# Longer fixed times for VectorE and ScalarE and a shorter one for GpSimd in the plan that orders an attention and rational-FFN kernel

## The chip, the cores and the metric

The kernel runs on one core of one Trainium2 chip. The metric is the device time of one execution in microseconds (us); the median of the runs is compared.

## The reference, cut to what matters

```python
def sm_attn(qq, kk, vv):                       # softmax attention, scale 1/sqrt(64)
    s = scale * np.matmul(qq, kk.transpose(0, 1, 3, 2))
    s = s - np.max(s, axis=-1, keepdims=True)
    a = np.exp(s)
    a = a / (np.sum(a, axis=-1, keepdims=True) + 1e-09)
    return np.matmul(a, vv)
p_packed = sm_attn(p, k, v)                    # q, k, v: 8 x 8 x 576 x 64; p: 8 x 8 x 32 x 64
out = sm_attn(q, p_packed, p_packed)
x = out.transpose(0, 2, 1, 3).reshape(4608, 512)
h = x @ w_in                                   # 512 x 2048
P = a[0] + a[1] * h + a[2] * h * h + a[3] * h * h * h
Q = 1.0 + np.abs(b[0]) * np.abs(h) + np.abs(b[1]) * h * h
g = P / (Q + 1e-6)
return g @ w_out                               # 2048 x 512
```

`q`, `k`, `v` and `p` are float32; the weights `w_in` and `w_out` come as float64 and go in as their 64-bit words.

## The kernel before

**How the work is cut.** The feed-forward part is cut into 128 units: batch (8), half of the batch's 576 rows (2 x 288), chunk of 256 of the 2048 hidden columns (8). In the names of tiles the unit's number stands in the middle: `Y0_115_1398` is buffer 0 of ring `Y` as unit 115 uses it; a name's last number counts all tiles. For each unit, `hidden` computes h into two PSUM banks (`h0`, `h1`), with twelve 128x288 matmuls from `AH`/`AL` (the attention's result, split into a high and a low float32r part) and `m`. ScalarE reads each bank three times: `Y` (a3 h + a2), `U` (|b h|) and `sq` (the square). VectorE then turns `Y` into the numerator with a multiply and a scalar-tensor-tensor (stt) per bank; the second of them is the last reader of the bank. GpSimd adds `sq` to `U`; ScalarE takes Ln and Exp of it (`V`, 1/Q); VectorE does three 128x576 operations to get g in `Y`; ScalarE casts it to `gh`, GpSimd subtracts for `gl`, and copies the columns of the batch's last rows to `G`. Three units later `acc_block` multiplies `gh`, `gl` with `w_out` (`w`) in twelve 128x512 matmuls into `acc`, whose sums leave through `o` every eight units. `remainder` does the rows in `G`.

**What lies between.** The attention of the next batch, and its `m_chunk` (`at<-win,ppT`, 16 small matmuls, then a ScalarE cast and a VectorE subtraction `m<-at,m`), are spread over the units as filler. The attention keeps its working tile in `kx`, a ring with one buffer: `kx<-nat` (VectorE transposes) brings k of the next batch into it, and the last reads of the previous batch are ScalarE's `AH<-kx` and GpSimd's `AL<-kx`. In the first units (up to about the tenth, "early") the weights' words are still being converted: VectorE `o<-o` operations on 128x1024 words, then a ScalarE cast and a GpSimd subtraction to `w`. Rings that matter here: `h` 2 banks in all (so unit n+1's h waits for unit n's stt on the same bank), `Y` 3, `U` 2, `sq` 1, `kx` 1, `o` 1, `at` 2.

**What sets the order.** Nothing is issued where it is written. Class `Planner` records all 7086 operations (`PlannedEngine`), finds from the tiles what must come before what (`edges`), and plans start times by list scheduling (`schedule`), with rounds that go through the program backwards to set each operation's rank; of 4 rounds the plan that ends first is kept (`order`). `issue` (line 216) then emits the operations by planned start. So almost every instruction has line 216, and each engine works its own list strictly in that order. A planned duration is `fixed + per * columns` by engine (`cost`), with the pair taken from `COST`:

```python
        fixed, per = self.COST[engine]
        ...
        return fixed + per * self.columns(aps[1] if name.startswith("reduce") else aps[0])
```

Of the kernel before, what the change touches and what calls it, by code (L numbers as in the profile page):

```python
# [31 lines left out]
class Planner:  # L32
# [4 lines left out]

    ENGINES = ("tensor", "vector", "scalar", "gpsimd", "sync")

    COST = {"vector": (70, 1.04), "scalar": (93, 0.83), "gpsimd": (215, 2.11), "tensor": (15, 0.417)}  # L40
    TRANSPOSE, F32 = (15, 0.834), (30, 1.667)
    WAY = {("vector", "vector"): 127, ("scalar", "scalar"): 143, ("tensor", "tensor"): 0, ("gpsimd", "gpsimd"): 0}
    WAY.update({(f"sync", x): 0 for x in ENGINES})
# [32 lines left out]
    def cost(self, engine, name, args, kwargs):  # L76
        if engine == "sync":
            return self.DMA_ISSUE
        fixed, per = self.COST[engine]
        if engine == "tensor":  # L80
# [875 lines left out]
```

## Time and profile before

| | |
|---|---|
| time, median of 3 runs | 804.35 us (803.67 to 804.96) |
| the profiled execution's own time | 803.09 us |
| its span | 801.3 us |
| mean granted TensorE clock | 0.97 of full speed |
| PE (TensorE matmul) busy | 745.9 us, 93% |
| DVE (VectorE) busy | 706.9 us, 88% |
| ACT (ScalarE) busy | 671.3 us, 84% |
| POOL (GpSimd) busy | 460.7 us, 57% |

The profile is one execution on the chip. Engine names are those of the table; busy time is the time in which at least one instruction of the engine is under way, and a share is of the span. The span leaves out what lies around it, 1.8 us here. A row of a timeline gives the start, the time, the engine, the operation with out<-in, and in brackets how long the engine stood idle before it and whose result ended the wait. Rows of one kind that follow each other closely are joined (x2 and more).

### The profile page before, as it was taken

The page shows a single profiled execution, that of the slowest core. Times are in us where ns is not written, and L with a number is a line of the kernel's source. Part 1 is how long each engine was busy: PE and PEld are TensorE (multiplying, and loading weights), DVE is VectorE, ACT ScalarE, POOL GpSimd, SP SyncE. Part 2 cuts the span into 40 slices and gives each one's busy share as a digit, 9 for nine tenths or more (in the row PEclk, how much of TensorE's full clock was granted, in tenths as well). Part 3 has the DMA queues.
Part 4 walks back from the last instruction along what each step waited for, and adds up shares of the span by engine and source line. Part 5 has one row for each costly group of instructions (what it writes and reads, how often), then busy time and mean ns, then how long its engine had stood idle before and what let it go on. Part 6 is the DMA issues. An engine that isn't in the chain of part 4 may idle for free.

```text
span 801.3 us, 15242 instructions
## 1 busy us (share of the span) xinstructions
PE 745.9 (93%) x5440; PEld 588.2 (73%) x5440; DVE 706.9 (88%) x1308; ACT 671.3 (84%) x1494; POOL 460.7 (57%) x462
## 2 busy tenths in 40 slices
PE   5587686899999999999999999999999999999997
PEld 4255464678878788678877888778877887778886
DVE  2999999898899789998899789998899789998883
ACT  5899988789888798889888798889788798998972
POOL 0006455565577555756568455855578555866663
PEclk9668899899999999999999999999999999999999
DMA  7983135002730208110720219010910123000001
GB/s 251 387 251 134 58 114 80 27 5 79 88 66 1 83 15 114 39 56 27 105 49 3 82 27 129 12 57 27 118 35 26 54 38 64 1 1 26 27 1 41
DMA packets 152029, 56.05 MB, mean 70 GB/s; under 512 B 122256, under 2 KB 141200, under 8 KB 151952
## 3 DMA queue, kind: packets, MB, share of 16 engines
q1 hardware_dynamic: 151952, 55.07, 29.9%
q8 instruction: 43, 0.70, 0.4%
q14 instruction: 34, 0.28, 0.1%
HBM read 45.62 MB, written 9.44 MB: 69 GB/s over the span
## 4 chain that ended last, share of the span: by engine, by line
PE 71%; DVE 12%; ACT 10%; DMA 3%; POOL 2%; issue 2%; SPq 1%; DVEq 0%
PE acc L216 36%; PE h L216 23%; PE at L216 13%; DVE Y L216 6%; ACT Y L216 2%; DVE w L216 2%; ACT m L216 1%; DMA w<-in_q_dram 1%; ACT U L216 1%; DVE small L216 1%; ACT V L216 1%; ACT w L216 1%; DVE V L216 1%; POOL gl L216 1%; ACT sq L216 1%
## 5 line engine op out<-in xcount | busy, mean ns | idle before, releaser
L216 PE MATMUL acc<-w,gh 128*128 128x512 f32 x1024 | 328.2, 402 | 9.9 <-ACT w L216 5.0
L216 PEld LDWEIGHTS acc<-w,gh 128*128 128x128 f32 x1024 | 185.6, 190 | 61.2 <-issue 9.7
L216 POOL TENSOR_TENSOR U<-U,sq 128x576 f32<-128x576 f32 x118 | 169.1, 1433 | 81.4 <-ACT U L216 52.1
L216 PE MATMUL h<-AH,m 128*128 128x288 f32 x1024 | 189.1, 306 | 13.6 <-DVE Y L216 12.5
L216 POOL TENSOR_TENSOR gl<-Y,gh 128x512 fp32r<-128x512 f32 x128 | 168.2, 1314 | 48.1 <-ACT gh L216 19.6
L216 PE MATMUL acc<-w,gl 128*128 128x512 f32 x512 | 192.2, 397 | 0.0
L216 PEld LDWEIGHTS h<-AH,m 128*128 128x128 f32 x1024 | 160.3, 193 | 43.3 <-DVE Y L216 29.2
L216 ACT ACTIVATE Y<-h,abS 128x288 f32<-128x288 f32 x256 | 125.1, 507 | 19.5 <-PE h L216 13.6
L216 DVE TENSOR_TENSOR Y<-Y,h 128x288 f32<-128x288 f32 x256 | 109.9, 445 | 27.3 <-ACT Y L216 9.9
L216 ACT ACTIVATE sq<-h 128x288 f32<-128x288 f32 x236 | 97.8, 416 | 42.4 <-PE h L216 33.7
L216 DVE SCALAR_TENSOR_TENSOR Y<-Y,abS,h 128x288 f32<-128x288 f32 x256 | 125.1, 506 | 2.3
L216 DVE SCALAR_TENSOR_TENSOR Y<-Y,abS,V 128x576 f32<-128x576 f32 x128 | 103.0, 805 | 22.5 <-ACT V L216 21.9
L216 PEld LDWEIGHTS acc<-w,gl 128*128 128x128 f32 x512 | 96.6, 189 | 27.9 <-issue 8.4
L216 PE MATMUL h<-AL,m 128*128 128x288 f32 x512 | 111.5, 299 | 0.0
L216 ACT ACTIVATE U<-h 128x288 f32<-128x288 f32 x256 | 98.6, 421 | 12.2 <-PE h L216 5.9
L216 POOL COPY G<-Y 128x64 f32<-128x64 f32 x128 | 32.2, 251 | 129.8 <-DVE Y L216 120.4
L216 ACT ACTIVATE V<-U,one 128x576 f32<-128x576 f32 x128 | 97.8, 764 | 5.3 <-DVE Y L216 5.1
L216 DVE SCALAR_TENSOR_TENSOR Y<-V,Y 128x576 f32<-128x576 f32 x128 | 95.8, 748 | 2.0
L216 DVE SCALAR_TENSOR_TENSOR V<-U,V 128x576 f32<-128x576 f32 x128 | 96.1, 751 | 0.0
L216 ACT CAST gh<-Y 128x512 fp32r<-128x512 f32 x128 | 80.9, 632 | 6.7 <-DVE Y L216 5.9
L216 ACT ACTIVATE V<-V 128x576 f32<-128x576 f32 x128 | 84.4, 660 | 0.5
L216 PEld LDWEIGHTS h<-AL,m 128*128 128x128 f32 x512 | 84.2, 192 | 0.2
(124 smaller groups left out, 828.3 us busy)
## 6 DMA issues: line engine op xcount, KB each, us to landing
out_dram<-o SPq DMA_DIRECT2D x15, 512.0 KB, 2.8
w<-in_moe_w_out_dram SPq DMA_DIRECT2D x14, 512.0 KB, 4.5
nat<-in_k_dram SPq DMA_DIRECT2D x48, 144.0 KB, 3.9
nat<-in_q_dram SPq DMA_DIRECT2D x48, 144.0 KB, 4.4
nat<-in_v_dram SPq DMA_DIRECT2D x24, 256.0 KB, 3.7
m<-in_moe_w_in_dram SPq DMA_DIRECT2D x8, 512.0 KB, 9.8
w<-in_moe_w_in_dram SPq DMA_DIRECT2D x8, 512.0 KB, 11.3
nat<-in_k_dram SPq DMA_DIRECT2D x4, 512.0 KB, 7.5
```

The lines of the kernel that those rows point to most:

```text
L216: getattr(getattr(self.nc, engine), name)(*args, **kwargs)
```

## The change

One line differs: the fixed part of the planned duration rises from 70 to 100 ns for VectorE and from 93 to 121 ns for ScalarE, and falls from 215 to 170 ns for GpSimd.

```diff
--- before.py
+++ after.py
@@ -37,7 +37,7 @@
 
     ENGINES = ("tensor", "vector", "scalar", "gpsimd", "sync")
 
-    COST = {"vector": (70, 1.04), "scalar": (93, 0.83), "gpsimd": (215, 2.11), "tensor": (15, 0.417)}
+    COST = {"vector": (100, 1.04), "scalar": (121, 0.83), "gpsimd": (170, 2.11), "tensor": (15, 0.417)}
     TRANSPOSE, F32 = (15, 0.834), (30, 1.667)
     WAY = {("vector", "vector"): 127, ("scalar", "scalar"): 143, ("tensor", "tensor"): 0, ("gpsimd", "gpsimd"): 0}
     WAY.update({(f"sync", x): 0 for x in ENGINES})
```

The recorded operations and what depends on what are the same in both kernels; so are the tile numbers. What differs is the order in which each engine has its instructions. Three places:

**VectorE, units 10 to 12, while the last weight words are converted** (`o0_2_263<-o0_2_263`, three rows; `kx` and `small` are the attention's, `m0_9` the early `m_chunk`'s). Before (the two transposes `kx0_2_141<-at0_49_278` and `kx0_2_141<-at1_50_279` stand right ahead of these rows, and the third `o` row right behind them):

```order
L216 SCALAR_TENSOR_TENSOR Y0_10_253<-Y0_10_253,abS_68,V0_10_252 128x576
L216 TENSOR_REDUCE small_73<-kx0_2_141 128x18
L216 SCALAR_TENSOR_TENSOR V0_10_252<-U1_10_251,V0_10_252 128x2x288
L216 SCALAR_TENSOR_TENSOR Y0_10_253<-V0_10_252,Y0_10_253 128x576
L216 TENSOR_TENSOR m0_9_298<-at0_51_299,m0_9_298 128x512
L216 TENSOR_TENSOR Y2_12_282<-Y2_12_282,h0_23_284 128x288
L216 TENSOR_REDUCE small_73<-kx0_2_141 128x18
L216 TENSOR_SCALAR o0_2_263<-o0_2_263 128x512
L216 TENSOR_TENSOR Y2_12_282<-Y2_12_282,h1_24_287 128x288
L216 SCALAR_TENSOR_TENSOR o0_2_263<-o0_2_263 128x512
L216 SCALAR_TENSOR_TENSOR Y2_12_282<-Y2_12_282,abS_68,h0_23_284 128x288
```

After:

```order
L216 SCALAR_TENSOR_TENSOR Y0_10_253<-Y0_10_253,abS_68,V0_10_252 128x576
L216 TENSOR_SCALAR o0_2_263<-o0_2_263 128x512
L216 SCALAR_TENSOR_TENSOR V0_10_252<-U1_10_251,V0_10_252 128x2x288
L216 SCALAR_TENSOR_TENSOR o0_2_263<-o0_2_263 128x512
L216 SCALAR_TENSOR_TENSOR Y0_10_253<-V0_10_252,Y0_10_253 128x576
L216 ISA o0_2_263<-o0_2_263,full0_3_264 128x512x2
L216 TENSOR_TENSOR Y2_12_282<-Y2_12_282,h0_23_284 128x288
L216 TENSOR_REDUCE small_73<-kx0_2_141 128x18
L216 SCALAR_TENSOR_TENSOR Y2_12_282<-Y2_12_282,abS_68,h0_23_284 128x288
L216 TENSOR_TENSOR Y2_12_282<-Y2_12_282,h1_24_287 128x288
L216 SCALAR_TENSOR_TENSOR Y1_11_267<-Y1_11_267,abS_68,V0_11_266 128x576
L216 SCALAR_TENSOR_TENSOR Y2_12_282<-Y2_12_282,abS_68,h1_24_287 128x288
```

The three `o` rows now stand between the last operations of unit 10; one of the two `small` reductions, the `m0_9` subtraction and the two transposes stand behind the operations of unit 12 shown here, where before they stood ahead of unit 12's first stt.

**VectorE, units 94 to 97, where k of the next batch comes in** (`kx0_8_1222<-nat`: four transposes into the one `kx` buffer). Before:

```order
L216 TENSOR_TENSOR Y2_96_1198<-Y2_96_1198,h0_191_1200 128x288
L216 TENSOR_TENSOR Y2_96_1198<-Y2_96_1198,h1_192_1201 128x288
L216 SCALAR_TENSOR_TENSOR Y2_96_1198<-Y2_96_1198,abS_68,h0_191_1200 128x288
L216 SCALAR_TENSOR_TENSOR Y2_96_1198<-Y2_96_1198,abS_68,h1_192_1201 128x288
L216 TENSOR_TENSOR full0_6_1184<-at0_169_1205,full0_6_1184 128x512
L216 SCALAR_TENSOR_TENSOR Y1_95_1187<-Y1_95_1187,abS_68,V0_95_1186 128x576
L216 STREAM_TRANSPOSE kx0_8_1222<-nat0_39_1118 128x576
L216 SCALAR_TENSOR_TENSOR V0_95_1186<-U0_95_1185,V0_95_1186 128x2x288
L216 STREAM_TRANSPOSE kx0_8_1222<-nat1_40_1129 128x576
L216 SCALAR_TENSOR_TENSOR Y1_95_1187<-V0_95_1186,Y1_95_1187 128x576
L216 TENSOR_TENSOR Y0_97_1208<-Y0_97_1208,h0_193_1210 128x288
L216 STREAM_TRANSPOSE kx0_8_1222<-nat0_39_1118 128x576
```

After:

```order
L216 STREAM_TRANSPOSE kx0_8_1222<-nat0_39_1118 128x576
L216 SCALAR_TENSOR_TENSOR Y1_95_1187<-Y1_95_1187,abS_68,h0_189_1189 128x288
L216 TENSOR_TENSOR Y1_95_1187<-Y1_95_1187,h1_190_1190 128x288
L216 STREAM_TRANSPOSE kx0_8_1222<-nat1_40_1129 128x576
L216 SCALAR_TENSOR_TENSOR Y1_95_1187<-Y1_95_1187,abS_68,h1_190_1190 128x288
L216 STREAM_TRANSPOSE kx0_8_1222<-nat0_39_1118 128x576
L216 TENSOR_TENSOR m1_30_1193<-at0_167_1194,m1_30_1193 128x512
L216 SCALAR_TENSOR_TENSOR Y0_94_1176<-Y0_94_1176,abS_68,V0_94_1175 128x576
L216 TENSOR_TENSOR m1_30_1193<-at1_168_1195,m1_30_1193 128x512
L216 SCALAR_TENSOR_TENSOR V0_94_1175<-U1_94_1174,V0_94_1175 128x2x288
L216 STREAM_TRANSPOSE kx0_8_1222<-nat1_40_1129 128x576
L216 SCALAR_TENSOR_TENSOR Y0_94_1176<-V0_94_1175,Y0_94_1176 128x576
```

The four transposes stood behind unit 96's operations on its `h` banks, the first of them behind both; now all four stand ahead of those (which follow as the next four rows), between unit 95's. At unit 64 all four have moved in the same way, at unit 32 three of the four. On GpSimd the second of the two subtractions `AL0_7_1136<-kx0_7_1046,AH0_9_1135`, which the first transpose waits for, now stands ahead of `gl0_93` and unit 95's addition `U0_95`; before, both stood behind those.

**ScalarE, unit 115, in the last batch.** Before:

```order
L216 ACTIVATE sq0_105_1399<-h0_229_1400 128x288
L216 ACTIVATE sq0_105_1399<-h1_230_1402 128x288
L216 ACTIVATE Y0_115_1398<-h0_229_1400,abS_68 128x288
L216 ACTIVATE Y0_115_1398<-h1_230_1402,abS_68 128x288
L216 ACTIVATE U0_115_1396<-h0_229_1400 128x288
L216 ACTIVATE U0_115_1396<-h1_230_1402 128x288
```

After:

```order
L216 ACTIVATE sq0_105_1399<-h0_229_1400 128x288
L216 ACTIVATE Y0_115_1398<-h0_229_1400,abS_68 128x288
L216 ACTIVATE sq0_105_1399<-h1_230_1402 128x288
L216 ACTIVATE Y0_115_1398<-h1_230_1402,abS_68 128x288
L216 ACTIVATE U0_115_1396<-h0_229_1400 128x288
L216 ACTIVATE U0_115_1396<-h1_230_1402 128x288
```

The square of the second bank stood ahead of the first bank's `Y`; now it stands behind it. Units 116 and 118 to 124 have the same exchange, unit 117 has not.

## Rows read from the trace of the kernel before

**Rows 1.** The page: busy time of each engine (us, share of the span, instructions), and one row of the costliest groups (busy us, mean ns of one, idle time before it).

```profile
PE 745.9 (93%) x5440; PEld 588.2 (73%) x5440; DVE 706.9 (88%) x1308; ACT 671.3 (84%) x1494; POOL 460.7 (57%) x462
...
L216 DVE TENSOR_TENSOR Y<-Y,h 128x288 f32<-128x288 f32 x256 | 109.9, 445 | 27.3 <-ACT Y L216 9.9
```

**Rows 2.** Busy time by stretch: PE, PEld (weight loads), DVE, ACT, POOL busy us (x instructions), the granted TensorE clock, the share of the DMA engines, GB/s.

```profile
100.00:150.00 50.00, 37.87 (x310) 27.40 (x308) 48.39 (x90) 40.68 (x82) 27.58 (x26) 0.93 0.37 78
150.00:200.00 50.00, 50.00 (x347) 41.20 (x348) 45.76 (x89) 43.91 (x105) 31.77 (x35) 1.00 0.14 44
584.00:607.00 23.00, 22.33 (x129) 18.08 (x128) 21.71 (x41) 21.28 (x48) 19.30 (x20) 1.00 0.06 24
705.00:755.00 50.00, 49.20 (x271) 41.46 (x264) 43.84 (x78) 43.66 (x102) 30.98 (x33) 1.00 0.03 11
```

**Rows 3.** The same view of two stretches of 10 us.

```profile
130.00:140.00 10.00, 4.96 (x51) 2.86 (x49) 9.97 (x18) 8.73 (x20) 5.74 (x7) 0.98 0.11 44
140.00:150.00 10.00, 6.36 (x35) 4.44 (x35) 8.43 (x16) 5.91 (x13) 5.17 (x5) 0.68 0.01 2
```

**Rows 4.** The chain of waits that ended last, followed inside 100 to 150 us: start, us, what.

```profile
141.76 0.43 DVE Y L216
...
142.24 2.53 PE h L216 x9
```

**Rows 5.** PE's timeline, 132 to 151 us.

```profile
134.95 1.09 PE L216 MATMUL at<-win,ppT 64*32 64x512 f32 x16
142.24 1.33 PE L216 MATMUL h<-AH,m 128*128 128x288 f32 x4 [6.20 <-DVE Y L216]
...
146.27 1.11 PE L216 MATMUL at<-win,ppT 64*32 64x512 f32 x16
...
149.91 0.73 PE L216 MATMUL acc<-w,gh 128*128 128x512 f32 x2 [1.40 <-ACT o L216]
```

**Rows 6.** VectorE's timeline, 126 to 152 us.

```profile
133.45 0.84 DVE L216 STREAM_TRANSPOSE kx<-at 128x288 f32<-128x288 f32 x2
...
134.91 0.74 DVE L216 TENSOR_REDUCE small<-kx 128x18 f32<-128x576 f32 x1
...
137.02 0.68 DVE L216 TENSOR_TENSOR m<-at,m 128x512 fp32r<-128x512 f32 x1
...
140.12 0.44 DVE L216 TENSOR_TENSOR Y<-Y,h 128x288 f32<-128x288 f32 x1
...
142.11 0.68 DVE L216 CUSTOM_DVE_ANT_0 o<-o,full 128x1024 uint16<-128x1024 uint16 x1
...
148.11 0.69 DVE L216 TENSOR_TENSOR m<-at,m 128x512 fp32r<-128x512 f32 x1 [1.50 <-ACT m L216]
...
150.44 0.81 DVE L216 SCALAR_TENSOR_TENSOR Y<-Y,abS,V 128x576 f32<-128x576 f32 x1 [0.36 <-ACT V L216]
```

**Rows 7.** VectorE's timeline, 603 to 618 us.

```profile
607.42 0.69 DVE L216 TENSOR_TENSOR m<-at,m 128x512 fp32r<-128x512 f32 x1 [0.71 <-ACT m L216]
...
611.25 0.82 DVE L216 TENSOR_TENSOR Y<-Y,h 128x288 f32<-128x288 f32 x2 [0.15 <-ACT U L216]
611.99 0.93 DVE L216 SCALAR_TENSOR_TENSOR Y<-Y,abS,h 128x288 f32<-128x288 f32 x2
...
614.16 0.77 DVE L216 STREAM_TRANSPOSE kx<-nat 128x576 f32<-128x576 f32 x1
614.86 0.73 DVE L216 SCALAR_TENSOR_TENSOR V<-U,V 128x576 f32<-128x576 f32 x1
```

**Rows 8.** PE's timeline in the same stretch: the first `h` matmuls of unit 97.

```profile
613.74 0.69 PE L216 MATMUL h<-AH,m 128*128 128x288 f32 x4
```

**Rows 9.** GpSimd's timeline in the same stretch.

```profile
607.57 2.84 POOL L216 TENSOR_TENSOR AL<-kx,AH 128x576 fp32r<-128x576 f32 x2
```

**Rows 10.** PE's timeline, 505 to 536 us: two waits.

```profile
522.15 0.73 PE L216 MATMUL acc<-w,gh 128*128 128x512 f32 x2 [0.45 <-ACT gh L216]
...
532.48 0.80 PE L216 MATMUL h<-AH,m 128*128 128x288 f32 x4 [0.36 <-DVE Y L216]
```

**Rows 11.** The timeline of all engines in the last batch, 713 to 725 us; 714.30 and 719.08 are the first `h` matmuls of units 115 and 116.

```profile
714.30 0.79 PE L216 MATMUL h<-AH,m 128*128 128x288 f32 x4
...
715.46 0.41 ACT L216 ACTIVATE sq<-h 128x288 f32<-128x288 f32 x1 [0.55 <-PE h L216]
...
716.18 0.41 ACT L216 ACTIVATE sq<-h 128x288 f32<-128x288 f32 x1 [0.30 <-PE h L216]
...
716.49 0.89 ACT L216 ACTIVATE Y<-h,abS 128x288 f32<-128x288 f32 x2
...
717.25 0.72 ACT L216 ACTIVATE U<-h 128x288 f32<-128x288 f32 x2
...
717.78 0.82 DVE L216 TENSOR_TENSOR Y<-Y,h 128x288 f32<-128x288 f32 x2 [0.56 <-ACT U L216]
...
718.51 0.93 DVE L216 SCALAR_TENSOR_TENSOR Y<-Y,abS,h 128x288 f32<-128x288 f32 x2
...
719.08 0.80 PE L216 MATMUL h<-AH,m 128*128 128x288 f32 x4 [0.19 <-DVE Y L216]
```

**Rows 12.** PE's timeline in the same stretch: the first `h` matmuls of unit 117.

```profile
723.29 0.73 PE L216 MATMUL h<-AH,m 128*128 128x288 f32 x4
```

**Rows 13.** PE's timeline, 750 to 760 us: the first `h` matmuls of unit 124.

```profile
755.70 0.81 PE L216 MATMUL h<-AH,m 128*128 128x288 f32 x4 [0.21 <-DVE Y L216]
```

## Prediction

> **What bounds the kernel now.** I read the busy times first, then the stretches, then the chain of waits, then the timelines of the places where the new order differs. The page shows PE busy for 93% of the span and VectorE for 88% [rows 1]. That average hides two regimes [rows 2]. From 100 to 150 us VectorE is busy for 48.39 of 50 us and PE for 37.87: VectorE sets the pace there. From 150 to 200 us PE is busy for all 50 us and VectorE has 4 us to spare, and later stretches look alike: 22.33 of 23 us from 584 to 607, 49.20 of 50 from 705 to 755. So after 150 us an earlier VectorE or ScalarE result is worth at most the idle time of PE that it ends, and a later one costs nothing until it eats the slack in front of PE. The change alters no instruction, only orders, so the sum is one of waits: which of PE's waits shrink, which appear.
>
> **The start (term A).** From 130 to 150 us PE works 4.96 and 6.36 us of each 10 us [rows 3], and the chain that ended last runs through VectorE up to the stt at 141.76, then through unit 13's h [rows 4]. Those h matmuls come after the longest wait here, 6.20 us for VectorE [rows 5]. The order now puts ahead of that stt: one reduction less (0.74), the subtraction m0_9 less (0.68), one multiply of the other bank less (0.44), the two transposes less (0.84), and the third conversion row more (0.68) [rows 6]. That is 2.70 - 0.68 = 2.02 us; each instruction starts about 0.08 us before the end of the one ahead (two multiplies take 0.82 us, and the next row starts 0.73 us after their start [rows 11]), and with four instructions fewer it is about 1.7 us. So h of unit 13 should start near 140.5 instead of 142.24.
>
> I don't count all of that. The instructions taken out from in front stand behind, before unit 14's first operation or soon after it, and from there VectorE has the same work behind it as before. What lasts is VectorE's idle time that the new order fills: 1.50 us in front of a subtraction m at 148.11, which waits for ScalarE's cast and now stands further back, and 0.36 us at 150.44 [rows 6]. That gives 1.9 us. The bounds: at best the 1.7 us, the 1.50 us and PE's 1.40 us wait at 149.91 [rows 5] all stay, 4.6 us; at worst nothing stays and the two groups of m_chunk matmuls, 1.09 and 1.11 us, which lay in PE's idle time (134.95) or beside it (146.27) [rows 5] and which the new order puts behind the accumulations of units 9 and 10, fall into PE's full stretch, +2.2. I take -1.9, near the middle.
>
> With PE's clock it goes the same way: it is granted 0.68 of full speed, between 1.2 and 2.4 GHz, in the ten microseconds with the 6.20 us wait, against 0.98 in the ten before [rows 3]; a wait of 4.5 instead of 6.2 us may leave it there or not, and I count nothing for it.
>
> **The transposes of k (term B).** Each takes 0.70 us of VectorE from its start to the next one's [rows 7], four are 2.8 us. Before, they lay behind unit 96's stt on its first bank, which ends about 611.99 + 0.51 = 612.50 (two with an overlap of 0.08 us take 0.93, so one (0.93 + 0.08) / 2), and unit 97's h starts at 613.74 [rows 7, 8]: slack 1.24 us. Now they lie ahead of it. They also fill VectorE's gaps at 607.42 (0.71) and 611.25 (0.15) [rows 7]. So PE's new wait is 2.8 - 0.86 - 1.24 = 0.7 us. A second wait can come on top: `kx` has one buffer, and the first transpose waits for GpSimd's second AL. Before, the pair of ALs took 607.57 to 610.41 [rows 9], over 3.7 us ahead of the first transpose at 614.16; now the transpose stands right behind unit 95's first multiply, ahead of the subtraction at 607.42 [rows 7] and so at least 6.7 us earlier, while the second AL is moved ahead of gl0_93 and unit 95's addition only, and unit 95's remaining h operations queue behind it. I bound that wait by nothing and by one AL, 2.84 / 2 = 1.42 us. A place thus costs 0 to 2.1 us, and I take 1.0. Units 64 and 96 have it; at unit 32 the fourth transpose stays behind, which leaves 2.1 - 0.86 - 1.24 = 0. Two places: +2.0, from 0 to +4.2; with the AL wait at all three, +5.6.
>
> **Waits that go (term C).** In units 77 to 82 and 45 to 50, the same transposes and m subtractions stand further back, behind unit operations. PE's two real waits there are 0.45 us for `gh` and 0.36 us for a VectorE result [rows 10], together 0.81, and 1.6 for both places. Units 84 to 86 get more VectorE work ahead in return, so I take half: -0.8, from -1.6 to 0.
>
> **The last batch (term D).** Units start 4.60 us apart (714.30 to 755.70, nine units), and the shortest spacing with the same matmuls, 719.08 to 723.29, is 4.21: 0.39 us per unit are not PE's own work [rows 11 to 13]. ScalarE waits 0.30 us at 716.18 for the second bank's h before its square, and only then does the two Ys and the two Us; the multiply at 717.78 waits 0.56 us for U, and 719.08 waits for VectorE [rows 11]. The new order does the first bank's Y in that gap (two take 0.76 us, from 716.49 to 717.25). So Y and U end 0.30 us earlier. Nine units have the exchange; where the spacing is already 4.2 nothing can come of it. Nine times 0.30 is 2.7, and I take a little over half: -1.5, from -2.7 to 0.
>
> **Does the table come nearer to the engines?** A 128x288 multiply lasts 445 ns in the mean [rows 1], and two of them with the next start take 0.73 us, 0.365 each [rows 11]. The old plan has 70 + 1.04 x 288 = 370 ns, the new one 400. As a length of a result the new number is nearer, as a length of occupation the old one is. A rule of the Trainium skill speaks here against the change ("Perfetto Trace Analysis", section "DVE / Act Engine Instruction"): the profiler's duration runs until the write is acknowledged, while the next instruction may begin to fetch when execution ends, so recorded durations overstate what an engine is held for. The trace agrees by the two numbers above. By it the new plan sees about 1308 x 30 ns = 39 us of VectorE work that isn't there, and its order is a redraw with no better aim: net zero, 804.35.
>
> **The sum**, against the profiled execution's own 803.09: -1.9 + 2.0 - 0.8 - 1.5 = -2.2, 800.9. The median shown is 1.26 above that execution, so I give the median as 802.1. A difference under about 0.2% (1.6 us) can't be told from no change.
>
> **Rivals.**
> - Nothing net: where PE is the bound, waits only change places. A falls to +0.3 (the m_chunk matmuls on PE's path take back the filled idle time, -1.9 + 2.2), C to 0, B and D stay: +0.8, 805.1; or, as a redraw, 804.35. For it: PE is full from 150 us on [rows 2]. Against it: PE's idle time in the last batch is real and has one cause.
> - Slower: the transposes wait for GpSimd's AL with VectorE's queue behind them, at all three places, 2.1 us each: +6.3 instead of +2.0, the other terms as forecast, +2.1, 806.5. It decides when a place costs more than 4.2 / 3 = 1.4 us. For it: VectorE is busy 21.71 of the 23 us ahead of the place [rows 2] and cannot absorb a wait. Against it: gaps of 0.86 us right behind [rows 7].
> - A larger gain: the start keeps its whole 4.6 us and D its 2.7: -4.6 + 2.0 - 0.8 - 2.7 = -6.1, 798.2. For it: the chain really runs through that stt. Against it: VectorE's later work is unchanged.
>
> **How the numbers follow.** Forecast 40%, its own range 800.5 to 803; larger gain 13%; nothing net 24%; slower 23%. The likeliest is 802.1. The range 797 to 808 reaches to both outer cases. Faster by over 0.2% (below 802.7): four fifths of the forecast's share and the larger gain, 0.45; slower by over 0.2% (above 806.0): the slower rival and some of nothing net, 0.27; the same 0.28.
>
> **What would show it.** A: the wait of 6.20 us before unit 13's h falls below 5, VectorE's 1.50 us gap ahead of the subtraction is gone, and PE is full from about 148. B: a wait of unit 97's h for VectorE, 0.5 to 2 us, and a VectorE wait for GpSimd's AL ahead of the first transpose, or none. C: no waits over 0.3 us where unit 77 to 82 run. D: ScalarE's Y ahead of its second square, and a mean spacing near 4.45 us from unit 115 to 124. The prediction is wrong if PE shows new waits in places that I haven't read, such as the first 100 us, where the orders differ most, or behind unit 125, where the last batch drains.

## The result and the profile after

The changed kernel is slower: 809.75 us (median of 6 runs, 808.47 to 811.29) against 804.71 of the kernel before in the same session, a ratio of 1.0069 with a 95% interval of 1.0057 to 1.0081, so about 5.5 us. The profiled execution took 809.4 us with a span of 807.5, 6.2 above the span of before. PE's busy time has grown by 2.8 us [rows 1], and the time in which it isn't busy by 3.4:

```profile
PE 748.7 (93%) x5440; PEld 588.4 (73%) x5440; DVE 705.2 (87%) x1308; ACT 668.9 (83%) x1494; POOL 467.1 (58%) x462
```

**Where PE waits behind 150 us.** The first block is the view of waits of the changed kernel, from 150 to 760 us, the second that of before: who waited for whom, us in total, times, the longest.

```profile
PE h L216 <- DVE Y L216: 8.9, 21, 0.8
PE acc L216 <- ACT gh L216: 1.2, 2, 0.6
PE at L216 <- POOL o L216: 0.8, 3, 0.3
```

```profile
PE h L216 <- DVE Y L216: 3.0, 9, 1.0
PE acc L216 <- ACT gh L216: 2.6, 7, 0.5
PE acc L216 <- ACT o L216: 1.4, 1, 1.4
```

PE's waits for a VectorE result in front of h have gone from 9 to 21 and from 3.0 to 8.9 us. The waits for `gh` have halved. The one for ScalarE's `o` (1.40 us, [rows 5]) ended at 149.91; the view lists it because its matmuls run past 150, and it belongs to the start. Without it the listed waits come to 5.6 us before and 10.9 after. They are small in the changed kernel, 0.2 to 0.8 us each, and those for h are spread from unit 20 to unit 118.

**The start.** The stretches 0 to 150, 50 to 100, 100 to 130 and 130 to 150 us, first of the changed kernel, then of before (columns as in [rows 2]):

```profile
0.00:150.00 150.00, 106.63 (x834) 75.04 (x835) 126.93 (x224) 121.07 (x240) 55.25 (x49) 0.85 0.56 170
50.00:100.00 50.00, 36.47 (x255) 24.24 (x254) 47.82 (x76) 46.15 (x96) 25.88 (x18) 0.82 0.38 121
100.00:130.00 30.00, 24.56 (x196) 19.57 (x195) 30.00 (x54) 23.57 (x49) 16.53 (x12) 0.94 0.40 96
130.00:150.00 20.00, 14.94 (x99) 11.36 (x98) 18.44 (x36) 16.07 (x37) 11.85 (x12) 0.91 0.30 56
```

```profile
0.00:150.00 150.00, 105.40 (x861) 74.37 (x861) 129.80 (x232) 123.89 (x245) 50.16 (x51) 0.84 0.55 170
50.00:100.00 50.00, 37.65 (x261) 27.84 (x262) 47.69 (x77) 45.93 (x97) 21.58 (x18) 0.82 0.38 122
100.00:130.00 30.00, 26.55 (x226) 20.10 (x225) 30.00 (x58) 26.04 (x51) 16.67 (x15) 1.00 0.58 115
130.00:150.00 20.00, 11.32 (x86) 7.30 (x84) 18.39 (x33) 14.64 (x32) 10.91 (x11) 0.83 0.06 23
```

From 130 to 150 PE works 14.94 us instead of 11.32. But from 100 to 130 it works 24.56 instead of 26.55, with its clock granted at 0.94 instead of 1.00, and from 50 to 100 it works 1.2 us less. Over all 150 us it is busy for 1.2 us longer, and has yet begun fewer matmuls, 834 against 861.

### The profile page after: what moved, and what is told of

The parts are those of the page before. It is cut to its first block, busy times and chain, and to the rows that moved or that the text cites. A ratio compares the mean times of both kernels' runs of the same rounds, so it can differ in the third digit from the quotient of the medians.

```text
span 807.5 us, 15287 instructions
## 1 busy us (share of the span) xinstructions
PE 748.7 (93%) x5440; PEld 588.4 (73%) x5440; DVE 705.2 (87%) x1308; ACT 668.9 (83%) x1494; POOL 467.1 (58%) x462
## 4 chain that ended last, share of the span: by engine, by line
PE 57%; DVE 19%; ACT 12%; DMA 4%; issue 4%; SPq 2%; POOL 2%; DVEq 0%; POOLq 0%; ACTq 0%
PE acc L216 28%; PE h L216 18%; PE at L216 11%; DVE Y L216 9%; ACT Y L216 2%; ACT V L216 2%; DVE w L216 2%; SPq L216 2%; DVE kx L216 2%; DVE small L216 2%; DVE V L216 2%; ACT U L216 2%; ACT sq L216 2%; DMA w<-in_moe_w_in_dram 1%; DMA w<-in_moe_w_out_dram 1%
## 5 line engine op out<-in xcount | busy, mean ns | idle before, releaser
L216 PE MATMUL acc<-w,gh 128*128 128x512 f32 x1024 | 319.9, 401 | 10.4 <-ACT w L216 8.4
L216 DVE TENSOR_TENSOR Y<-Y,h 128x288 f32<-128x288 f32 x256 | 108.1, 445 | 39.3 <-ACT U L216 28.0
L216 DVE SCALAR_TENSOR_TENSOR Y<-Y,abS,h 128x288 f32<-128x288 f32 x256 | 122.9, 504 | 1.5
L216 POOL COPY G<-Y 128x64 f32<-128x64 f32 x128 | 40.9, 320 | 115.1 <-DVE Y L216 106.0
L216 ACT ACTIVATE U<-h 128x288 f32<-128x288 f32 x256 | 96.9, 425 | 4.1 <-DVE V L216 2.3
```

The source lines that it names most:

```text
L216: getattr(getattr(self.nc, engine), name)(*args, **kwargs)
```

## The experiments

All times are ratios of the runs to the runs of before that were taken with them, with 95% intervals; 0.1% is 0.8 us. "Span" is that of the one profiled execution (801.3 for before).

**One number at a time.** Three tables, each with one of the three numbers changed.

```diff
-    COST = {"vector": (70, 1.04), "scalar": (93, 0.83), "gpsimd": (215, 2.11), ...
+    COST = {"vector": (100, 1.04), "scalar": (93, 0.83), "gpsimd": (215, 2.11), ...   # e1_vector
+    COST = {"vector": (70, 1.04), "scalar": (121, 0.83), "gpsimd": (215, 2.11), ...   # e2_scalar
+    COST = {"vector": (70, 1.04), "scalar": (93, 0.83), "gpsimd": (170, 2.11), ...    # e3_gpsimd
```

> Only VectorE's fixed time goes from 70 to 100 ns. Theory one (the loss comes from where VectorE's other work now stands in front of the operations that free h banks, so it is VectorE's number that decides): most of the change's +5 us, 807 to 810. Theory two (the loss comes from ScalarE's order, whose other work now stands between its reads of an h bank): near before, 803 to 806. Theory three (no part decides; each new table draws another order and the old one happened to be a good draw): any time between 800 and 812, and no sum over the three parts.

Measured: 1.0023 (1.0013 to 1.0033).

> Only ScalarE's fixed time goes from 93 to 121 ns. Theory one (VectorE's number): near before, 803 to 806. Theory two (ScalarE's number): 807 to 810, with VectorE waiting for ScalarE's U as in the changed kernel. Theory three (a draw): anything from 800 to 812.

Measured: 1.0025 (1.0016 to 1.0035).

> Only GpSimd's fixed time goes from 215 to 170 ns. Theories one and two: near before, 803 to 806, since GpSimd is busy for 58% and its number is now nearer to its pace. Theory three (a draw): anything from 800 to 812, and again other than the rest of the change would leave.

Measured: 1.0041 (1.0028 to 1.0055). No number carries the loss alone, and the one that I took for harmless costs most. That speaks against the first two theories. The sum of the three, 0.89% where the whole is 0.69%, decides nothing: the intervals allow the two to be equal. The later runs test the third theory directly.

**The start alone, and everything but the start.** Both plans are made in one kernel, and the order is taken from one of them up to the first h matmul of unit 17, then from the other.

```diff
     def issue(self):
-        for i in self.order():
+        plans = {}
+        plans["old"] = self.order()
+        self.COST = self.NEW
+        plans["new"] = self.order()
+        head, tail = plans["new"], plans["old"]      # e4_head_new; e11_head_old: the other way round
...
+        head = head[: at[0]]                         # at[0]: the first operation on h0_33
+        done = set(head)
+        for i in head + [i for i in tail if i not in done]:
```

> The changed kernel's order up to the first h matmul of unit 17 (about 170 us), the order of before from there. If the start is a third of the loss, as unit 17 starting 1.8 us later in the changed kernel suggests: 806 to 807. If the later start is only PE work that was done ahead (PE was busy 1.2 us longer in the first 150 us of the changed kernel): 804.5 to 805.5. If my forecast of a gain at the start held: 802 to 803.5.

Measured: 1.0015 (1.0005 to 1.0025), span 802.9, 1.6 above before. From unit 20 to the end the distance of this run to the one before stays at 1.5 to 1.7 us, since every engine then does the same in the same order. One span doesn't size the start: executions whose order is still that of before reach unit 14 from 1.0 us earlier (e11_head_old) to 0.8 later (e12_swap) than the profiled one of before. The times do: the start is a real loss, of 1.2 us (0.4 to 2.0).

> The order of before up to unit 17, the changed kernel's from there: the rest without the start. The whole is 5.5 us and the start alone 1.2, so 4.3 above before if the two add up: 808 to 809.5. If the seam costs or gives work of its own, as it did in the mixed order: off by up to 3 us.

Measured: 1.0074 (1.0060 to 1.0089), span 805.7, 4.4 above before. By the spans start and rest add up (1.6 + 4.4 = 6.0 of 6.2); by the times they come to 7.1 of 5.5, which their intervals just allow. Most of the loss lies behind unit 17.

**The last batch alone.** The same edit with the order of before up to unit 114 (`h0_227`) and the changed one from there.

> The order of before up to the first h matmul of unit 114 (about 710 us), the changed kernel's order from there: term D alone. My forecast was -1.5 us, so 802. The traces of the two kernels say that the changed one loses about 1.1 us behind unit 113: 804.5 to 805.

Measured: 0.9995 (0.9986 to 1.0004), span 801.5. The last batch as a whole neither gains nor loses: neither number was right. Units 115 to 124 stand 4.67 us apart in this run against 4.60 before, and what that costs is made up behind unit 124.

**The exchange on ScalarE alone.** The order of before, and in units 115 to 124 ScalarE's reads of h in the sequence of the changed kernel.

```diff
...
+        for n in range(115, 125):
+            own = [k for k, i in enumerate(row) if self.unit(self.ops[i][1][0]) == n]
+            for k, i in zip(own, sorted((row[k] for k in own), key=at.get)):
+                row[k] = i
```

> The order of before, with ScalarE's exchange alone in units 115 to 124 (the first bank's Y ahead of the second bank's square). My term D as it was argued: 1.5 us faster, 802 to 803, with units 4.4 us apart. If the Y waits for its buffer, whose last reader is GpSimd's gl three units back, as the changed kernel's trace says: no gain, 803.5 to 805, ScalarE waiting about 0.2 us for gl ahead of Y.

Measured: 1.0010 (1.0002 to 1.0019), no gain. The view of ScalarE's waits from 700 to 760 us, the two largest groups of this run and the largest of before:

```profile
ACT sq L254 <- PE h L254: 4.2, 9, 0.6
ACT Y L254 <- POOL gl L254: 2.0, 7, 0.4
```

```profile
ACT sq L216 <- PE h L216: 5.7, 13, 0.6
```

The wait for GpSimd's `gl`, which the kernel before doesn't have there at all, has come with this exchange alone. Its 2.0 us take back the 1.5 that the squares wait less.

**Stretches of different plans put together.** In the run of e2_scalar the distance to before shrank from 5.3 us at unit 17 to 0.4 at unit 113. So I took that plan between the two, and the order of before at both ends.

```diff
+    PIECES = [('old', 'h0_33'), ('sca', 'h0_225'), ('old', None)]   # 'sca': ScalarE at 121
...
```

> The order of before up to unit 17, the order of the plan with ScalarE's number alone (121) up to unit 113, the order of before behind it. In that plan's own run the distance to before fell from 5.3 us at unit 17 to 0.4 at unit 113. If what a stretch costs stays with its order (as the head's 1.6 us did), this one is 4.9 us faster than before: 798 to 799.5. If the gain was only catching up with a late start, nothing is left of it: 803 to 804.

Measured: 1.0044 (1.0030 to 1.0058), slower than either of its parts. The reading behind it was wrong: this run too is 4.1 us behind at unit 17 and 0.8 at unit 105, and then 4.4 at unit 113, at the seam. When unit 17 starts says how much attention work PE has done by then as well as how late it is. What a plan does early it needn't do later, and a seam pays the difference. The start of a unit measures lost time only where both orders have done the same work up to it, as behind unit 20 in e4_head_new.

**No other work inside the h chain.** On ScalarE and VectorE, from unit 17 on, whatever stands between a unit's first and last operation on its h banks goes behind the last one, where the dependences allow; in the changed kernel, and in the one before.

```diff
+                part = row[own[0] : own[-1] + 1]
+                new = [i for i in part if u[i] == n] + [i for i in part if u[i] != n]
...
+                tried = {**lists, e: row[: own[0]] + new + row[own[-1] + 1 :]}
+                if self.merged(tried, order):
+                    lists = tried
```

> The changed kernel's order, and from unit 17 on all that ScalarE and VectorE have between a unit's first and last operation on its h banks is put behind the last one, wherever the dependences allow. If PE's new waits for VectorE come from other work standing inside that chain: most of the 4.3 us behind unit 17 is back, 805 to 806.5. If they come from how PE's own filler is spread over the units, or the order is one draw among many: still 808 to 812.

Measured: 1.0591 (1.0575 to 1.0606).

> The same rule on the order of before, which has more such work inside the chain (154 rows on ScalarE and 134 on VectorE, against 94 and 79 in the changed one). If that work costs time: faster than before, 800 to 803. If what is pushed back is missed as badly elsewhere: 804 to 810.

Measured: 1.0696 (1.0677 to 1.0714). Both are over 47 us slower. PE's waits in e9_gather_new from 150 to 800 us, the three largest groups:

```profile
PE h L259 <- DVE Y L259: 10.2, 15, 2.2
PE at L259 <- DVE kx L259: 6.4, 5, 1.6
PE at L259 <- ACT kx L259: 5.4, 5, 1.4
```

The waits for h haven't even fallen (10.2 us in 15 waits, the longest 2.2), and others have come, for the attention's transposes and exponentials. So other work inside the chain is not in itself the loss: moving it out costs far more than the change studied, and the kernel before, which has more of it, is the faster one. Single rows can still cost something there (term C below has one); which of them do, these two runs can't say, since they move all of them at once.

**Two nanoseconds.** Tables beside the old one and beside the new one, one number moved by 2 ns. The edit is again one number; the table behind the expectations shows it.

> VectorE's fixed time goes from 70 to 72 ns only, which says nothing else about the engine. Theory one (a number that is too long puts the wrong work first): the time of before, 802.5 to 804.5. Theory three (a draw: any change of a number gives another order, and the one of before was a good draw): another time, by some us and most likely slower, 804.5 to 808.

> ScalarE's fixed time goes from 93 to 95 ns only. The same two theories: 802.5 to 804.5 if the size of the number matters, another time by some us (804.5 to 808, or faster than 802) if each table is a draw.

> The table of before with GpSimd at 217 in place of 215. If the numbers count: 802.5 to 804.5. If it is a draw: anything from 801 to 811.

> The table of before with VectorE at 68 in place of 70. If the numbers count: 802.5 to 804.5. If it is a draw: anything from 801 to 811; with VectorE at 72 it was 3.6 us slower, and a slope through 70 would make 68 faster by as much, 800.

> The changed kernel's table with VectorE at 102 in place of 100. If the size of the numbers makes the loss: as slow as the changed kernel, 808.5 to 811. If each table is a draw: anything from 801 to 811, as likely off the changed kernel by 3 us as near it.

> The changed kernel's table with ScalarE at 123 in place of 121. The same: 808.5 to 811 if the numbers count, anything from 801 to 811 if it is a draw.

> The changed kernel's table with VectorE at 98 in place of 100. If the new numbers cost something on top of the scatter: 806 to 811, as the three runs so far around that table. If only the scatter is there, as wide as around the old table: as likely 801 to 806 as above it.

> The changed kernel's table with GpSimd at 172 in place of 170. The same two: 806 to 811 if the numbers cost something on top, as likely 801 to 806 if there is only scatter.

Measured (fixed times of VectorE, ScalarE, GpSimd in ns; the last column adds up PE's waits from 150 to 760 us as the view lists them, for before and e14_new_scal123 with one of 1.4 and 0.8 us that ended just ahead of 150):

| kernel | table | ratio | 95% interval | PE's waits, us |
|---|---|---|---|---|
| e8_scal95 | 70, 95, 215 | 0.9972 | 0.9960 to 0.9984 | 3.7 |
| e15_gps217 | 70, 93, 217 | 0.9989 | 0.9980 to 0.9999 | 6.0 |
| before | 70, 93, 215 | 1 | | 7.0 |
| e16_vec68 | 68, 93, 215 | 1.0039 | 1.0026 to 1.0052 | 6.8 |
| e7_vec72 | 72, 93, 215 | 1.0048 | 1.0032 to 1.0065 | 8.3 |
| e13_new_vec102 | 102, 121, 170 | 1.0037 | 1.0026 to 1.0047 | 5.6 |
| e17_new_vec98 | 98, 121, 170 | 1.0047 | 1.0033 to 1.0061 | 9.3 |
| e18_new_gps172 | 100, 121, 172 | 1.0052 | 1.0038 to 1.0066 | 7.0 |
| after | 100, 121, 170 | 1.0069 | 1.0057 to 1.0081 | 10.9 |
| e14_new_scal123 | 100, 123, 170 | 1.0079 | 1.0063 to 1.0095 | 12.6 |

Two things follow. First, one order is a draw: 68 and 72 for VectorE are both slower than 70, by 0.39% and 0.48%, and 95 for ScalarE is faster than 93 by 0.28%; a change that says nothing new about an engine moves the time by as much as most of the change studied here. Second, that is not all: the five tables around the old one have a mean of 1.0010 and reach from 0.9972 to 1.0048, the five around the new one a mean of 1.0057 and reach from 1.0037 to 1.0079. Only two of the old five are as slow as the new group's fastest. So the new numbers seem to cost something on top of the scatter: the means differ by 0.47%, with a standard error of about 0.16% if the tables count as independent draws, which neighbours with mostly the same numbers need not be. The old table's own order is a slightly better draw than its neighbours' mean, and at the start it is the best of all: by the profiled runs none of the other twelve tables reaches unit 20 as early (0.35 to 4.15 us later). Between unit 20 and unit 116, by which all have done the same matmuls, the old five change by -0.9 us in the mean and the new five by +2.8, so the groups part there rather than at the start. What in the plans makes the new group slower isn't settled: no run here takes a single cause out of it.

The draws are not quite blind. The planner's own end for each order (`self.end`, worked out from each kernel, no measurement) is 772.8 us for e8_scal95, 778.3 for before, 778.5 for e15_gps217, 781.0 for e16_vec68 and 782.7 for e7_vec72: the order of the measured times but for two neighbours that lie 0.1% apart. In the new group it is 798.1 for e17_new_vec98, 799.9 for e18_new_gps172, 802.4 for e13_new_vec102, 802.5 for after and 803.0 for e14_new_scal123: the two latest are the two slowest, but e13_new_vec102, the fastest, doesn't fit. Between the groups the ends can't be compared, since the table itself sets them.

The fastest, e8_scal95, beats both kernels: 802.17 us against 804.32 of before with it. Its waits of PE, in the same view as above:

```profile
PE h L216 <- DVE Y L216: 3.4, 11, 0.7
PE acc L216 <- ACT gh L216: 0.3, 1, 0.3
```

## Why the prediction was wrong

I forecast -2.2 us in four terms at four places; measured are about +5.5. By the spans: start +1.6 (forecast -1.9), the units between +4.2 (4.4 less the 0.2 of the last batch; forecast +2.0 - 0.8 = +1.2), last batch +0.2 (forecast -1.5).

**Term A, the start: the idle time that was to be filled was moved.** All that I had named as signs came: the 6.20 us wait [rows 5] has become these two on PE's timeline, VectorE's 1.50 us gap ahead of the subtraction is gone, and PE runs without a wait from 145.08 to unit 20.

```profile
137.87 0.80 PE L216 MATMUL h<-AH,m 128*128 128x288 f32 x4 [1.38 <-DVE Y L216]
...
144.06 1.22 PE L216 MATMUL acc<-w,gh 128*128 128x512 f32 x2 [3.68 <-ACT w L216]
```

PE worked 3.6 us more between 130 and 150 us (14.94 against 11.32, above), and unit 14 started 1.6 us earlier than before (151.85 against 153.46), where I had reckoned 1.9 to last. But PE has done less by then. Two of `m_chunk`'s four groups of matmuls had run before unit 14 in the kernel before (134.95 and 146.27, [rows 5]); in the changed kernel none had, and they follow in PE's full stretch:

```profile
155.84 1.09 PE L216 MATMUL at<-win,ppT 64*32 64x512 f32 x16
...
161.87 1.09 PE L216 MATMUL at<-win,ppT 64*32 64x512 f32 x16
```

With these two (1.02 us each to the next start) and one accumulation matmul (0.23) still to do, unit 14 is not 1.6 us ahead but some 0.7 behind, and unit 17 starts 1.8 us late. This is the worst case of my own bounds, the +2.2. I took -1.9 as "near the middle" of -4.6 and +2.2, which is -1.2.

The failing step: I counted VectorE's idle 1.50 and 0.36 us [rows 6] as filled for good, by "the same work behind it as before". From 126 to 152 us VectorE waits 1.85 us in the changed kernel, against 1.86 before, only elsewhere:

```profile
133.72 0.81 DVE L216 SCALAR_TENSOR_TENSOR Y<-Y,abS,V 128x576 f32<-128x576 f32 x1 [0.34 <-ACT V L216]
...
136.57 0.82 DVE L216 TENSOR_TENSOR Y<-Y,h 128x288 f32<-128x288 f32 x2 [0.18 <-ACT U L216]
...
150.34 0.45 DVE L216 TENSOR_TENSOR Y<-Y,h 128x288 f32<-128x288 f32 x1 [1.33 <-ACT Y L216]
```

And I took this place for the start. The orders differ from the first units on: units 11 and 12 started over 4 us late, and unit 13, forecast for 140.5, came at 145.08. PE lost 2.0 us of work from 100 to 130 and 1.2 from 50 to 100, of which nothing stood in the sum; and busy time at a lower granted clock is less work (four of h's matmuls take 1.33 us at 142.24 [rows 5], in the stretch granted 0.68 [rows 3], and 0.69 at 613.74 [rows 8]). How the start's loss divides between these, the runs don't itemise. I had named the first 100 us as what could make the forecast wrong, and put no price on them.

**Term B, the transposes: the mechanism didn't occur.** VectorE around the first transpose, GpSimd's second AL and unit 97's h in the changed kernel:

```profile
609.64 0.45 DVE L216 TENSOR_TENSOR Y<-Y,h 128x288 f32<-128x288 f32 x1 [0.67 <-ACT U L216]
610.01 0.77 DVE L216 STREAM_TRANSPOSE kx<-nat 128x576 f32<-128x576 f32 x1
...
617.85 0.92 DVE L216 SCALAR_TENSOR_TENSOR Y<-Y,abS,h 128x288 f32<-128x288 f32 x2
```

```profile
608.51 1.46 POOL L216 TENSOR_TENSOR AL<-kx,AH 128x576 fp32r<-128x576 f32 x1
```

```profile
619.34 0.69 PE L216 MATMUL h<-AH,m 128*128 128x288 f32 x4
```

AL ends at 608.51 + 1.46 = 609.97, and the transpose starts at 610.01, right behind a multiply that had itself waited 0.67 us for ScalarE's U: nothing is added by AL. Unit 97's h starts at 619.34 with no wait, 1.0 us after the stt that frees its bank (617.85 + 0.51). From unit 95's first multiply to unit 96's stt VectorE took 8.21 us (609.64 to 617.85) where it had taken 7.36 before (604.63 to 611.99 on the timeline of [rows 7]): of the 2.8 us moved in, 1.95 went into VectorE's gaps, of which I had counted 0.86, and the 0.85 left is less than the slack of 1.24. Forecast +2.0 for two places; at this one no wait of PE came of it, and PE has none in front of units 65 and 33 either. VectorE has no wait for AL in front of the first transpose at any of the three places.

**Term C, waits that go: they doubled.** Of the two waits of [rows 10] the one for `gh` has gone, and the one in front of unit 82's h has grown from 0.36 to 0.65 us:

```profile
537.35 0.79 PE L216 MATMUL h<-AH,m 128*128 128x288 f32 x4 [0.65 <-DVE Y L216]
```

In units 77 to 82 and 45 to 50 together PE waits 3.3 us where it had waited 1.6: I forecast 0.8 less, and it is 1.7 more. The failing step was to count the waits that go and not those that the new order brings. The largest, at unit 78:

```profile
508.61 0.70 PE L216 MATMUL h<-AH,m 128*128 128x288 f32 x4
...
509.69 0.41 ACT L216 ACTIVATE sq<-h 128x288 f32<-128x288 f32 x1 [0.66 <-PE h L216]
...
510.00 0.58 ACT L216 CAST m<-at 128x512 fp32r<-128x512 f32 x1
...
510.46 0.52 ACT L216 ACTIVATE Y<-h,abS 128x288 f32<-128x288 f32 x1
...
511.53 0.74 ACT L216 ACTIVATE U<-h 128x288 f32<-128x288 f32 x2
...
512.61 0.74 DVE L216 TENSOR_TENSOR Y<-Y,h 128x288 f32<-128x288 f32 x2
...
513.27 0.92 DVE L216 SCALAR_TENSOR_TENSOR Y<-Y,abS,h 128x288 f32<-128x288 f32 x2
...
513.83 0.79 PE L216 MATMUL h<-AH,m 128*128 128x288 f32 x4 [0.70 <-DVE Y L216]
```

ScalarE does a cast of `m` between the first bank's square and its Y (510.00), so U ends at 512.27, the multiply follows at 512.61, the stt at 513.27, and PE, whose own work for this unit has ended, waits 0.70 us. The h spacing is 5.22 us where PE had 5.39 us of work between the same two units in the kernel before (503.49 to 508.88): the work that filled it stands elsewhere now. It is what my rival "nothing net" said of PE-bound stretches, waits that change places, only that it was worse than net zero: 12 more waits for h from 150 to 760 us.

**Term D, the last batch: a buffer that I didn't check.** All engines, unit 119 and the start of unit 120:

```profile
739.36 0.80 PE L216 MATMUL h<-AH,m 128*128 128x288 f32 x4
739.78 1.31 POOL L216 TENSOR_TENSOR gl<-Y,gh 128x512 fp32r<-128x512 f32 x1
...
740.53 0.41 ACT L216 ACTIVATE sq<-h 128x288 f32<-128x288 f32 x1 [0.56 <-PE h L216]
...
741.12 0.89 ACT L216 ACTIVATE Y<-h,abS 128x288 f32<-128x288 f32 x2 [0.19 <-POOL gl L216]
...
742.20 0.72 ACT L216 ACTIVATE U<-h 128x288 f32<-128x288 f32 x2
...
742.72 0.82 DVE L216 TENSOR_TENSOR Y<-Y,h 128x288 f32<-128x288 f32 x2 [0.44 <-ACT U L216]
...
743.06 1.43 POOL L216 TENSOR_TENSOR U<-U,sq 128x576 f32<-128x576 f32 x1 [0.48 <-ACT U L216]
...
744.02 0.80 PE L216 MATMUL h<-AH,m 128*128 128x288 f32 x4
744.45 1.30 POOL L216 TENSOR_TENSOR gl<-Y,gh 128x512 fp32r<-128x512 f32 x1
```

The first bank's Y could start behind the square at 740.84 (0.31 later), and the ScalarE exchange had put it there. But it waits for GpSimd: ring Y has three buffers, and the last reader of this one, three units back, is `gl`, which ends at 739.78 + 1.31 = 741.09. Y starts at 741.12. Before, Y started at 716.49 [rows 11], when its buffer was already free, so the order of before hid this wait behind the second square. The loop through GpSimd (Y, U, addition, `gl`, next Y) takes 4.66 us, and so does the spacing of these two units, from 739.36 to 744.02. From unit 115 to 124 the units stand 4.68 us apart in the mean, where I forecast 4.45 and the kernel before had 4.60. e12_swap shows the wait for `gl` and the missing gain in isolation (4.63 us apart).

The price was too high as well. I read 4.21 us as the spacing "with the same matmuls", but these 4.21 us hold 11 accumulation matmuls, and the 4.95 behind them 13. The shortest spacing with all 12 is 4.43 us (728.24 to 732.67 on PE's timeline of before). By that measure 0.17 us per unit was not PE's own work, where I had read 0.39: 1.5 us for nine units, so that my bound of 2.7 was out of reach.

**The rivals.** The side was that of "slower", but not its mechanism: it had GpSimd's AL at three places with 806.5, and the wait for AL isn't there. What was weighed under "Does the table come nearer to the engines?" gave "a redraw with no better aim". The scatter of the tables bears out the redraw, but not its net of zero: the mean around the new table is 0.57% above before. That numbers nearer to what an engine is held for make the better plan isn't shown either: GpSimd's new number was nearer to its occupation (170 + 2.11 x 576 = 1385 ns, and in the block above the addition at 743.06 is followed by `gl` at 744.45, 1.39 us later; the old number gave 1430), and it alone cost 0.41%.

**The step behind all four** is that I read four places of an order that differs throughout, and let the rest count as zero. PE's waits for h in the changed kernel run from unit 20 to unit 118, and 10 of the 21 lie at units that no term named (20, 29, 30, 43, 52, 53, 60, 92, 110 and 111); at 0.2 to 0.8 us each I saw none of them in the order. The chance of slower, 0.27, and a range that ended at 808 were narrower even than the terms themselves: their upper bounds, +2.2 and +5.6, add up to 812.

## What to carry to other kernels

Where a planner's table changes every engine's order, the four places that can be read don't bound the effect: run the same plan with a number moved by a few nanoseconds, and take that scatter (here from -0.3 to +0.5%) as the range before any mechanism is priced. A table is better or worse only as a group of neighbours, so compare groups, and keep the best draw; the plan's own end can say which neighbours to run first. A unit that starts earlier is a gain only if the engine has done the same work by then. When an operation is moved ahead of a wait, look up each thing it needs, the buffer it writes included, and the engine that frees that buffer.

## What the runs showed that I had not expected

In the changed kernel the spacing between units 119 and 120 is not set by the engine that is busiest in the last batch (PE, whose work for a unit has fitted into 4.43 us, above) but by a loop through the least busy one: GpSimd's addition and `gl`, 2.7 us of a 4.66 us cycle, in series with ScalarE. And PE's granted clock was 0.94 of full speed from 100 to 130 us, a stretch with three waits of 1.3 to 1.4 us, against 1.00 before, where no wait there was over 0.8 us; no run takes the two apart.
